# A convolution and a gated two-layer product on one core: the second product in 26 block products in place of 20, with some block sums on GpSimd

## The chip, the core and the metric

The kernel runs on one core of a Trainium2 chip. The core has TensorE (PE, matrix products into PSUM), VectorE (DVE), ScalarE (ACT), GpSimd (POOL) and SyncE (SP, which issues DMAs). The metric is device time in microseconds (us) of one execution, as the median of the runs. The kernel before takes 2314.07 us (three runs, 2314.03 to 2314.65).

## The reference

```python
# x: 8 x 4096 x 192, weight: 8 heads x 7 taps, w_in: 192 x 2048, w_out: 2048 x 192
w = softmax(weight, axis=-1)                   # per head
conv[b, s, c] = sum_k w[head(c), k] * x_pad[b, s + k, c]     # causal, 7 taps
h = conv.reshape(32768, 192) @ w_in
g = h * (1.0 / (1.0 + np.exp(-1.702 * h)))
out = g @ w_out                                # 32768 x 192, float32
```

A depthwise causal convolution of 7 taps, a product up to 2048 features, the quick gelu g = h·sigmoid(1.702h), and a product back to 192. All is float32.

## The kernel before

The tokens are worked off in 32 chunks ("big" in the code, `N_BIG`), each of 1024 tokens: 512 (`TOK`) from one half of the batch and 512 from the other. The first chunk is computed plainly, mixed with the preparation of the weights (`first_step`, `second_first`). Each of the other 31 passes through these stages:

1. **Convolution of the next chunks.** `transpose_x` turns the input with VectorE. The channels come in three blocks c = 0, 1, 2 of 64. Block 0 is done by ScalarE (`tap_times`: seven scaled copies) and GpSimd (`add_tap`: six adds of 128x512); blocks 2 and 1 are done by VectorE (`conv`, seven operations each). Then GpSimd forms eight sums of 128x256 (`sums_c`), and DMAs copy each half of the partitions to the other half (`cross`).
2. **Two hidden stages**, `hidden` with v = 0 and 1: h = conv · w_in by a fast scheme with 21 products (`TERMS`), each of four TensorE instructions in the trace. ScalarE copies PSUM banks into `room` (`copy2`), VectorE combines them (`sum2`), and ScalarE writes the gelu into `g` (`gelu`).
3. **The second product**, `second`: `w_out` and `g` are cut into blocks and multiplied by a scheme with 20 block products, each over five rows of 128 features; the sixteenth row is multiplied plainly. TensorE works in rounds: three matmuls with 32 columns of weights each make a step of the main product, and a fourth, beside them in the last 32 columns, a step of one of the side products (`side_product`, `go`). A round is 256 tokens wide, and there are 81 per chunk. VectorE forms sums of blocks of g (128x1280) ahead of the rounds that read them, and joins the products (96x256) into the four outputs, which it turns (`turn`) into `osbs` for the store.

Each engine works off its own queue in the order in which the program issues it; semaphores tie the queues together. The order within `second` is written out by hand: the sums, `go`, joins and `done` stand in the order of issue. Work that fits between (convolution, transposes) is handed out by `work` with a budget in us, and ScalarE's taps by `next_tap` in the last rounds. All six GpSimd adds of block 0 are issued behind the last of the seven tap copies. `prepare` lists the VectorE and GpSimd work of a chunk, `need` forces what is due. The sums of `w_out` (`w_form`) are made once, at the start, by ScalarE copies (`begin_forms`) and accumulating DMAs that GpSimd issues (`add_forms`).

What the steps of the prediction touch: L494 (VectorE's conv step), L501 (ScalarE's tap), L505 (GpSimd's tap add), L388 and L390 (`add_up`, GpSimd's `sums_c`), L607 (`copy2`), L611 (`sum2`), L598 and L600 (gelu), L867 (every matmul of `second`), L881 (copy of a side product), the sums of g in `hidden` and `second` (L649 to L930), the joins (L908 to L972) and L819 (`turn`).

## Time and profile before

| | |
|---|---|
| median of three runs | 2314.07 us (2314.03 to 2314.65) |
| span of the profiled execution | 2312.2 us, 1.87 below that median; its own time is not listed apart |
| granted TensorE clock | 1.000 |
| TensorE, matmul | 2304.8 us busy |
| VectorE | 2005.1 us busy, 2819 instructions |
| ScalarE | 1376.9 us busy, 2554 instructions |
| GpSimd | 432.4 us busy, 451 instructions |
| matmuls of the hidden stages (L577) | 852.5 us into the slots, 405.4 us into the sums |
| sums of g, 128x1280, VectorE | 16 lines x 31, 1.48 us each |
| conv step, 128x512, VectorE (L494) | x378, 0.803 us in the mean |
| tap copy, 128x512, ScalarE (L501) | x180 into g, 0.719 us |
| tap add, 128x512, GpSimd (L505) | x180, 1.360 us in the mean |
| sum of the convolution, 128x256, GpSimd (L390) | x180, 0.732 us |

The span runs from the first to the last instruction of one execution. An engine's busy time is what its instructions cover; matmuls overlap in the pipeline, so TensorE's says only that it always had work. A line of the timeline gives the start and the duration in us, the engine, the source line, the operation, and the tiles it writes and reads with their shapes; a bracket at its end gives the idle time before it and what ended that. The duration of an instruction runs from where its engine took it up to its end, so a wait for a resource inside the instruction is part of it.

### The profile page before, as it was taken

Reading aid. Unit: us, or ns where it says so; the run is one execution under the profiler, and the core shown is the slowest. Engines: PE = TensorE matmul, PEld = TensorE weight load, DVE = VectorE, ACT = ScalarE, POOL = GpSimd, SP = SyncE. Lnnn points to the kernel's source line nnn. Section 1 sums busy time; section 2 is a strip of 40 time slices with the busy share of each in tenths; the row PEclk is TensorE's granted clock in tenths of the full one; section 3 lists DMA queues with packets and bytes.
Section 4 is the critical chain, followed back from the end, with each engine's and each line's share of the span. In section 5 each row is a group of like instructions: output and inputs, shape, how many; then the busy total and the mean of one; then the engine's idle time right before and its main releaser. Section 6 shows DMA issues by size and latency. Waiting matters only on the chain.

```text
span 2312.2 us, 60320 instructions
## 1 busy us (share of the span) xinstructions
PE 2304.8 (100%) x25982; PEld 1217.8 (53%) x25982; DVE 2005.1 (87%) x2819; ACT 1376.9 (60%) x2554; POOL 432.4 (19%) x451
## 2 busy tenths in 40 slices
PE   9999999999999999999999999999999999999999
PEld 5355555555555555555555555555555555555556
DVE  8898889888898888898888988889888898888877
ACT  7555665566655556555566555665565655556644
POOL 0311222102221022211122211222102221022200
PEclk9999999999999999999999999999999999999999
DMA  8632322223221233112331132321223321231010
GB/s 185 121 67 60 70 52 47 56 57 70 65 48 43 57 70 70 42 43 58 70 70 43 44 69 57 70 53 45 57 57 70 68 45 43 57 70 45 17 43 16
DMA packets 199899, 137.99 MB, mean 60 GB/s; under 512 B 109008, under 2 KB 190544, under 8 KB 195664
## 3 DMA queue, kind: packets, MB, share of 16 engines
q1 hardware_dynamic: 197072, 130.98, 25.7%
q0 software_dynamic: 1728, 2.95, 0.8%
q8 instruction: 204, 3.34, 0.6%
q14 instruction: 63, 0.52, 0.1%
q10 hardware_dynamic: 832, 0.20, 0.0%
HBM read 53.15 MB, written 25.17 MB: 34 GB/s over the span
## 4 chain that ended last, share of the span: by engine, by line
PE 99%; ACT 0%; DVE 0%; DMA 0%; issue 0%; SPq 0%; DVEq 0%; ACTq 0%
PE slot L577 35%; PE slot L867 33%; PE sums L577 16%; PE sums L867 14%; PE slot L746 2%; DMA xin<-in_x_dram 0%; ACT conv_t L1029 0%; DVE xt L471 0%; DVE conv_t L494 0%; SPq L99 0%; ACT conv_t L354 0%; ACT conv_t L353 0%; DVE osbs L819 0%; ACT conv_t L523 0%; ACT conv_t L1025 0%
## 5 line engine op out<-in xcount | busy, mean ns | idle before, releaser
L577 PE MATMUL slot<-conv_t,w_in_s 64*128 64x512 f32 x3740 | 852.5, 590 | 0.3 <-DVE w_in_s L373 0.3
L867 PE MATMUL slot<-g,w_form 128*32 128x256 f32 x6700 | 772.5, 379 | 0.0
L577 PEld LDWEIGHTS slot<-conv_t,w_in_s 64*128 64x128 f32 x3740 | 369.0, 187 | 432.1 <-issue 386.9
L505 POOL TENSOR_TENSOR conv_t<-conv_t,g 128x512 f32<-128x512 f32 x180 | 244.8, 1360 | 1448.6 <-ACT conv_t L501 1436.8
L867 PEld LDWEIGHTS slot<-g,w_form 128*32 128x32 f32 x6700 | 399.6, 110 | 134.9 <-ACT g L598 23.5
L867 PE MATMUL sums<-g,w_form 128*32 128x256 f32 x3530 | 461.8, 379 | 0.0
L867 PE MATMUL slot<-g,w_out_s 128*32 128x256 f32 x4432 | 442.0, 379 | 0.0
L577 PE MATMUL sums<-conv_t,w_in_s 64*128 64x512 f32 x1660 | 405.4, 591 | 0.3 <-DVE w_in_s L373 0.3
L600 ACT ACTIVATE g<-room 128x1024 f32<-128x1024 f32 x310 | 324.5, 1073 | 90.9 <-DVE room L611 90.9
L494 DVE SCALAR_TENSOR_TENSOR conv_t<-xt,cw,conv_t 128x512 f32<-128x512 f32 (+1 forms) x390 | 309.3, 793 | 10.1 <-ACT conv_t L492 3.2
L867 PEld LDWEIGHTS slot<-g,w_out_s 128*32 128x32 f32 x4432 | 226.0, 110 | 97.5
L867 PEld LDWEIGHTS sums<-g,w_form 128*32 128x32 f32 x3530 | 233.3, 110 | 65.6
L607 ACT COPY room<-slot 128x512 f32<-128x512 f32 x434 | 231.5, 602 | 57.3 <-PE slot L577 57.3
L577 PEld LDWEIGHTS sums<-conv_t,w_in_s 64*128 64x128 f32 x1660 | 165.7, 187 | 189.1 <-issue 154.1
L598 ACT ACTIVATE g<-slot 128x512 f32<-128x512 f32 x334 | 179.7, 590 | 88.8 <-PE slot L577 88.8
L881 ACT COPY room<-slot 32x256 f32<-32x256 f32 x245 | 89.8, 367 | 205.8 <-PE slot L867 200.2
L867 PE MATMUL sums<-g,w_out_s 128*32 128x256 f32 x1706 | 205.3, 379 | 0.0
L867 PE MATMUL slot<-room,w_form 128*32 128x256 f32 x2340 | 182.1, 379 | 0.0
L611 DVE TENSOR_TENSOR room<-slot,room 128x512 f32<-128x512 f32 x248 | 156.1, 680 | 20.4 <-ACT room L607 20.4
L611 DVE TENSOR_TENSOR room<-room,sums 128x512 f32<-128x512 f32 x124 | 79.1, 679 | 70.2 <-PE sums L577 70.2
L611 DVE TENSOR_TENSOR room<-room,slot 128x512 f32<-128x512 f32 x124 | 79.1, 678 | 64.5 <-PE slot L577 64.5
L607 ACT COPY room<-sums 128x512 f32<-128x512 f32 x186 | 100.0, 591 | 58.8 <-PE sums L577 58.8
(212 smaller groups left out, 2665.5 us busy)
## 6 DMA issues: line engine op xcount, KB each, us to landing
xin<-in_x_dram SPq DMA_DIRECT2D x240, 180.0 KB, 4.1
conv_t<-conv_t SPq DMA_DIRECT2D x62, 512.0 KB, 6.2
out_dram<-osbs SPq DMA_DIRECT2D x186, 128.0 KB, 2.6
conv_t<-conv_t SPq DMA_DIRECT2D x62, 256.0 KB, 3.1
conv_t<-conv_t SPq DMA_DIRECT2D x62, 64.0 KB, 4.5
xin<-in_x_dram SPq DMA_DIRECT2D x16, 160.0 KB, 3.3
w_form<-w_out_s POOLq DMA_DIRECT2D x7, 240.0 KB, 4.1
osbs<-in_moe_w_out_dram SPq DMA_DIRECT2D x2, 768.0 KB, 8.3
```

Source lines behind the costliest of these rows:

```text
L494: vec.scalar_tensor_tensor(out=dst, in0=src, scalar=tap, in1=dst, op0=ALU.mult, op1=ALU.add)
L505: nc.gpsimd.tensor_add(dst, dst, tap_home(big, k))
L577: nc.tensor.matmul(slot[h], w_in_s[halves[h], a, v * P : (v + 1) * P], src, start=first, stop=True, skip_group_check=True,)
L598: act.activation(g[:, n, i + h, :], src[h], AF.Gelu_apprx_sigmoid)
L600: act.activation(g[:, n, i : i + 2, :], src, AF.Gelu_apprx_sigmoid)
L607: act.copy(bank(dst, h), bank(src, h))
L611: op(*(bank(t, h) for t in (dst, a, b)))
L746: nc.tensor.matmul(chunk(bank, c), w[:, chunk_cols(c)], t, start=first and i == 0, stop=not more and i == len(steps) - 1, skip_group_check ...
L867: nc.tensor.matmul(dst, w, t, start=first, stop=last, skip_group_check=True)
L881: act.copy(to, d)
```

## The change

- **The second product** goes by 26 products of blocks of four rows (16 = 4·4 rows, no row left over), and takes 78 rounds per chunk where it took 81. `g` is laid out anew as blocks of 4 rows by 256 tokens; `gelu` writes it with other strides. 19 of the products are main, 6 side, and one (form 8) is split between the two.
- **The sums of g** are 28 per chunk, of 128x1024 each, in place of 16 of 128x1280. Six of them are in-place adds on GpSimd ("acc" in the lists; the description given with the change speaks of eight): one in the second hidden stage and five inside the second product. The other 22 stay on VectorE: five in the hidden stage (`EARLY_G`), 17 in the second product.
- **The order** within `second` is a list, `PLAN`, that is worked off item by item: "sum" and "join" go to VectorE, "acc" to GpSimd, "seed" is a ScalarE copy of a value into another PSUM place, "go" n issues n rounds of the main product begun by "main", with the side product begun by "side" beside it, "tap" issues one convolution tap, "cross" one piece of the DMA copies.
- **Convolution block 2** moves from VectorE to ScalarE and GpSimd (`prepare_taps`, `tap`): 14 taps and 12 adds per chunk where there were 7 and 6. Each add is issued right behind its copy, into one of four places. Seven taps are issued in the last rounds of the second product, seven in the first hidden stage (`taps_at`). VectorE keeps block 1.
- **The DMA copies** `cross` of a chunk are cut into pieces of three blocks, issued at six places of `PLAN`.
- **The sums of w_out** are 19 GpSimd adds and six ScalarE negations at the start, with no accumulating DMAs.

```diff
-    NS, ND = 3, 5
-    assert len(PAIRS) * 4 == NF == NS * ND + 1
-    g = consts.tile([P, 2, NF, TOK], F32)
-    ROW = {1: 2, 2: 0, 3: 1}
-    COL = {1: (0, 0), 2: (0, 1), 3: (1, 1), 4: (1, 0)}
+    NG = 4
+    assert len(PAIRS) * 4 == NF == NG * NG
+    g = consts.tile([P, NG, 2, 2, NG, T], F32)
     def block(r, j):
-        n, o = COL[j]
-        i = ND * ROW[r]
-        return g[:, n, i : i + ND, o * T : (o + 1) * T]
-    def rest(j):
-        n, o = COL[j]
-        return g[:, n, NF - 1 :, o * T : (o + 1) * T]
+        return g[:, r, j // 2, j % 2, :, :]
+    def row(n, i):
+        return g[:, i // NG, n, :, i % NG, :]
...
+    ROOMS = (1, 2, 3)
+    SPOTS = 2 + len(ROOMS)
+    KEPT = (4, 0)
+    def spot(i):
+        if i >= SPOTS:
+            return block(*divmod(i - SPOTS, NG))
+        flat = osbs[:, i * BLK : (i + 1) * BLK] if i < 2 else room[:, ROOMS[i - 2], :]
+        return flat.rearrange("p (k t) -> p k t", k=NG)
+    KEPT_LATE, TAP_SPOTS = 3, (16, 15)
...
+    SUMS_O = [
+        (8, 7, "+", 6), (9, 5, "+", 7), (10, 2, "+", 6), (11, 3, "-", 5), (12, 3, "-", 6), (13, 3, "+", 7),
...
-    def begin_forms(items):
-        for dst, src, sign in items:
-            if sign == 1:
-                act.copy(form(dst), of_form(src))
-            else:
-                act.mul(form(dst), of_form(src), -1.0)
     def add_forms(items):
-        for dst, src in items:
-            nc.gpsimd.dma_start(out=form(dst), in_=of_form(src), accum_op=ALU.add)
+        for dst, a, op, b in items:
+            add_up(form, dst, a, op, b, eng=nc.gpsimd)
+    def end_forms():
+        add_forms(SUMS_O_LATE)
+        for i in TURN_O:
+            act.mul(form(i), form(i), -1.0)
...
-    def tap_times(big, k):
-        dst = tap_home(big, k) if k else own(big)[:, 0:2, :]
-        act.mul(dst, conv_src(big, 0, k), cw[:, 0, k : k + 1])
-    def add_tap(big, k):
-        dst = own(big)[:, 0:2, :]
-        nc.gpsimd.tensor_add(dst, dst, tap_home(big, k))
+    def tap(big, c, k):
+        dst = own(big)[:, 2 * c : 2 * c + 2, :]
+        home = tap_home(big, c, k) if k else dst
+        act.mul(home, conv_src(big, c, k), cw[:, c, k : k + 1])
+        if k:
+            nc.gpsimd.tensor_add(dst, dst, home)
...
+    def cross_now(early, big, b0, b1):
+        if early or big == 1:
+            cross(big, b0, b1)
+        else:
+            pieces.extend((big, b, min(b + 3, b1)) for b in range(b0, b1, 3))
+    def cross_piece():
+        if pieces:
+            cross(*pieces.pop(0))
...
-        yield from convs(2, 0) if big == 1 else convs(2, 1)
+        yield from convs(2, 0) if big == 1 else convs(1)
...
-        for k in (*range(1, K), 0):
-            yield "", 1.0, lambda k=k: tap_times(big, k)
-        for k in range(1, K):
-            yield "", 0.0, lambda k=k: add_tap(big, k)
+        for c in (0, 2):
+            for k in range(K):
+                yield "", 1.0, lambda c=c, k=k: tap(big, c, k)
...
+        dst = g[:, i // NG, n, :, i % NG : i % NG + 2, :]
...
+        def taps_at(n):
+            for _ in range(0 if v else n):
+                next_tap()
+        def early(i):
+            for item in EARLY_G[i] if v else ():
+                sum_g(*item)
         if v:
             pe(z, 7, first=True)
             give(True, big)
-        pe(sums, 12)
-        copy2(k15, sums)
-        pe(x, 5, 17)
+        if v:
+            pe(sums, 12)
+            copy2(k15, sums)
+            pe(x, 5, 17)
+        else:
+            pe(x, 5)
+            pe(sums, 12)
+            copy2(k15, sums)
+            pe(x, 17)
+            taps_at(1)
...
-            vec.tensor_add(t_s, block(2, 1), block(2, 4))
-            vec.tensor_sub(block(2, 1), block(2, 1), block(3, 1))
-        work(2.6 if v else 1.2)
+        early(1)
+        if not v or big == 1:
+            work(1.2)
         pe(sums, 13)
...
+        early(2)
...
-        if v:
-            vec.tensor_sub(t_a, block(2, 3), block(3, 3))
+        early(3)
...
-        if v:
-            vec.tensor_add(block(2, 3), block(2, 2), block(2, 3))
-            vec.tensor_sub(t_8, t_s, block(3, 1))
...
+    EARLY_G = [
+        [(6, 6, "-", 10)], [(1, 7, "-", 6), (1, 1, "-", 11)], [(0, 5, "+", 6), (8, 0, "acc")],
+        [(2, 9, "-", 0)],
+    ]
+    PLAN = [
+        ("side", 13, 16, "k0"), ("main", 1, 5, "p2", 1), ("go", 4), ("sum", 14, 14, "-", 18),
+        ("main", 16, 10, "p3", 0), ("go", 2), ("sum", 7, 8, "-", 7), ("go", 1), ("cross",), ("go", 1),
+        ("main", 0, 14, "p0", 1), ("go", 1), ("sum", 5, 11, "-", 19), ("go", 1), ("seed", "p4", "p2", 1),
+        ("go", 1), ("seed", "k1", "p3", 1), ("go", 1), ("sum", 8, 8, "-", 16), ("seed", "p5", "k1", 1),
+        ("side", 19, 1, "k1"), ("acc", 14, 13), ("main", 18, 0, "p2", 0), ("go", 3), ("sum", 6, 8, "-", 6),
+        ("go", 1), ("main", 5, 8, "p1", 0), ("go", 1), ("sum", 4, 5, "-", 10), ("go", 1), ("cross",),
+        ("seed", "k2", "p2", 1), ("go", 2), ("sum", 0, 0, "+", 5), ("main", 14, 2, "p2", 0), ("go", 2),
+        ("acc", 15, 4), ("go", 1), ("join", "k3", "p1", "+", "k0"), ("go", 1), ("sum", 11, 7, "+", 11),
+        ("side", 11, 17, "k0"), ("main", 23, 4, "p5", 0), ("go", 3), ("sum", 8, 6, "-", 13),
+        ("seed", "k4", "p2", 1), ("go", 1), ("cross",), ("seed", "p2", "k3", 1), ("main", 17, 6, "p1", 0),
+        ("go", 1), ("sum", 5, 20, "-", 12), ("go", 1), ("seed", "k5", "p5", 1), ("go", 1), ("acc", 7, 10),
+        ("go", 1), ("sum", 20, 20, "-", 11), ("main", 22, 11, "p2", 0), ("go", 2), ("seed", "k6", "p1", 1),
+        ("go", 1), ("seed", "p1", "k2", 1), ("go", 1), ("join", "k7", "k1", "+", "k6"),
+        ("side", 8, 8, "k1", 2, 4), ("main", 2, 5, "p4", 0), ("go", 1), ("sum", 13, 18, "+", 4), ("go", 2),
+        ("cross",), ("sum", 6, 9, "-", 5), ("go", 1), ("acc", 12, 9), ("main", 20, 0, "p1", 0), ("go", 2),
+        ("join", "k2", "k7", "-", "p4"), ("side", 6, 13, "k8"), ("go", 1), ("join", "k2", "k2", "-", "p2"),
+        ("go", 1), ("sum", 15, 15, "-", 16), ("main", 9, 6, "p4", 0), ("go", 3),
+        ("join", "k9", "p1", "+", "k5"), ("go", 1), ("join", "k10", "p0", "-", "k9"), ("main", 3, 15, "p2", 0),
+        ("go", 1), ("cross",), ("acc", 18, 14), ("go", 1), ("seed", "p1", "k1", 1), ("sum", 5, 7, "+", 15),
+        ("tap",), ("go", 2), ("main", 21, 7, "p2", 0), ("go", 1), ("sum", 6, 14, "+", 6), ("go", 1), ("tap",),
+        ("side", 7, 20, "k1"), ("go", 2), ("sum", 6, 6, "-", 17), ("main", 10, 14, "p0", 0), ("go", 2),
+        ("tap",), ("seed", "k5", "p2", 1), ("cross",), ("join", "k10", "k10", "+", "k8"), ("go", 2),
+        ("join", "p2", "p4", "+", "k3"), ("main", 8, 8, "p1", 0, 0, 2), ("go", 1),
+        ("join", "k8", "k9", "+", "k5"), ("tap",), ("go", 1), ("join", "k8", "k7", "-", "k8"),
+        ("main", 4, 6, "p4", 0), ("go", 1), ("turn", 1, 0, 1, "k10"), ("go", 1),
+        ("join", "k3", "p1", "+", "k6"), ("go", 1), ("tap",), ("join", "k3", "p0", "-", "k3"), ("go", 1),
+        ("join", "k6", "k0", "-", "p0"), ("side", 8, 5, "k0"), ("main", 15, 12, "p2", 0), ("go", 2),
+        ("join", "k7", "k4", "-", "p4"), ("go", 1), ("tap",), ("join", "k7", "k7", "+", "k3"), ("go", 1),
+        ("join", "k2", "k2", "-", "k1"), ("main", 12, 18, "p3", 0), ("go", 1), ("turn", 0, 0, 0, "k7"),
+        ("go", 1), ("join", "k6", "k6", "+", "p4"), ("tap",), ("go", 1), ("turn", 1, 1, 1, "k2"), ("go", 1),
+        ("turn", 1, 0, 0, "k6"), ("store", 0, 0), ("main", 24, 19, "p5", 0), ("go", 2), ("final",),
+        ("join", "k1", "p3", "-", "k3"), ("go", 1), ("turn", 0, 0, 1, "k1"), ("store", 0, 1), ("go", 1),
+        ("join", "k2", "p2", "-", "k4"), ("turn", 0, 1, 1, "k2"), ("store", 1, 1),
+        ("join", "k1", "p5", "+", "k5"), ("turn", 0, 1, 0, "k1"), ("join", "k8", "k8", "+", "k0"),
+        ("turn", 1, 1, 0, "k8"), ("store", 1, 0),
+    ]
+    def sum_g(dst, a, op, b=None):
+        if op == "acc":
+            nc.gpsimd.tensor_add(spot(dst), spot(dst), spot(a))
+        else:
+            add_up(spot, dst, a, op, b)
+    SIDE_HALF = (0, 0, 1, 0, 1, 0, 1)
...
+        mains, sides = (bs[0], bx[0], by[0]), (bx[1], bs[1], by[1])
+        side, count = [], [0]
...
+        def begin_side(f, s, to, *ks):
+            steps = product(f, s, *ks)
+            for c in range(NC):
+                turns, i = divmod(count[0], NC)
+                h = SIDE_HALF[turns]
+                count[0] += 1
+                dst = sides[i][n3:, h * T : (h + 1) * T]
+                for k, (w, t) in enumerate(steps):
+                    end = k == len(steps) - 1
+                    side.append((dst, w[:, chunk_cols(c)], t, k == 0 and h == 0, end and chunk(value(to), c)))
+        def begin_main(f, s, to, first, *ks):
+            now.update(steps=product(f, s, *ks), to=value(to), first=bool(first))
+        def go(n):
+            for _ in range(n):
+                w, t = now["steps"].pop(0)
                 for c in range(NC):
+                    one_matmul(chunk(now["to"], c), w[:, chunk_cols(c)], t, now["first"], not now["steps"])
+                now["first"] = False
                 d, ws, ts, st, to = side.pop(0)
                 one_matmul(d, ws, ts, st, to is not False)
                 if to is not False:
                     act.copy(to, d)
+        def seed(dst, src, sign):
+            if sign == 1:
+                act.copy(value(dst), value(src))
+            else:
+                act.mul(value(dst), value(src), -1.0)
+        def out_turn(m, n, o, src):
+            turn(m, n, blocks(value(src)), slice(o * T // Q, (o + 1) * T // Q))
+        def out_store(n, o):
+            if last:
+                queues = (nc.sync, nc.scalar) if o else (nc.scalar, nc.sync)
+                store(big, n, o, queues + queues[0:1])
+                return
+            stored[n] += 1
+            if stored[n] == 2:
+                store(big, n)
+        ops = dict(
+            sum=sum_g, acc=lambda d, a: sum_g(d, a, "acc"), main=begin_main, side=begin_side, go=go, seed=seed,
+            join=lambda d, a, op, b: add_up(value, d, a, op, b), turn=out_turn, store=out_store,
+            tap=next_tap, cross=cross_piece, final=final,
+        )
+        for item in PLAN:
+            ops[item[0]](*item[1:])
+        assert not side and not now["steps"] and count[0] == NC * len(SIDE_HALF)
+        while pieces:
+            cross_piece()
```

## The prediction

> **What bounds the kernel now.** I read the page's busy shares, the chain that ended last, stretches of one chunk, and then single instructions where GpSimd meets VectorE.
>
> The page, parts 1 and 4:
>
> ```profile
> PE 2304.8 (100%) x25982; PEld 1217.8 (53%) x25982; DVE 2005.1 (87%) x2819; ACT 1376.9 (60%) x2554; POOL 432.4 (19%) x451
> ...
> PE 99%; ACT 0%; DVE 0%; DMA 0%; issue 0%; SPq 0%; DVEq 0%; ACTq 0%
> ```
>
> TensorE is never idle and is the whole chain, so a TensorE round taken away is time saved, as long as the operands still arrive. Whether they do is read from the second-product stage (988.2 to 1023.2 us is one). Busy time by engine in two stretches, the stage and the change to the next chunk:
>
> ```profile
> 988.00:1022.00 34.00, 34.00 (x630) 20.46 (x632) 32.59 (x45) 16.04 (x36) 0.00 (x0) 1.00 0.17 41
> 1022.00:1033.00 11.00, 11.00 (x71) 5.12 (x64) 9.59 (x15) 5.97 (x12) 9.97 (x9) 1.00 0.35 74
> ```
>
> In the stage VectorE (third engine column) is busy 32.59 of 34.00 us and GpSimd (the fifth) not at all. So TensorE is the bound there with VectorE 4% behind it. GpSimd works only in the second stretch. The chunk's start shows what the two do to each other (timeline: start, us, engine):
>
> ```profile
> 98.11 0.77 DVE L494 SCALAR_TENSOR_TENSOR conv_t<-xt,cw,conv_t 128x512 f32<-128x512 f32 x1
> 98.41 1.60 POOL L505 TENSOR_TENSOR conv_t<-conv_t,g 128x512 f32<-128x512 f32 x1
> 98.92 1.64 DVE L494 SCALAR_TENSOR_TENSOR conv_t<-xt,cw,conv_t 128x512 f32<-128x512 f32 x1
> 100.09 1.60 POOL L505 TENSOR_TENSOR conv_t<-conv_t,g 128x512 f32<-128x512 f32 x1
> ...
> 1022.40 1.28 POOL L505 TENSOR_TENSOR conv_t<-conv_t,g 128x512 f32<-128x512 f32 x1 [49.19 <-ACT conv_t L501]
> 1022.63 1.34 DVE L959 TENSOR_TENSOR room<-room 96x256 f32<-96x256 f32 x1
> 1023.89 0.41 DVE L964 TENSOR_TENSOR spare<-spare,slot 96x256 f32<-96x256 f32 x1
> ```
>
> The reader should see three things. A VectorE operation with two SBUF inputs waits for a running GpSimd add: L959, of a shape that takes 0.415 us elsewhere (L949), takes 1.34 and ends at 1023.97, 0.29 after the add's end (1022.40+1.28). One with a PSUM input does not (L964, 0.41 us, during the next add). And they take turns: the add at 98.41 is 1.60 long, not 1.28; it ends at 100.01 and the conv behind it at 100.56. The next add ends at 101.69, so one such pair, each of 512 elements, takes 1.68 us.
>
> **The change, part by part.** Durations are from this execution, span 2312.2 us; the median run is 1.87 us above it, which I leave as it is. One chunk of before: two successive chunks on the chain are 142.71 us apart (690.76 to 833.47), so 71.36. There are 31.
>
> *Rounds.* 81 rounds take 988.2 to 1023.2, 35.0 us: 0.432 each. Three fewer: −1.30 us a chunk, −40.2 in all.
>
> *VectorE's list.* Sixteen sums of 1280 elements (1.48 us each; 1.40 from start to start in a row, L896 to L897) become 22 of 1024. The 2048-element sums (L762, 2.28) and 1280 give 1.05 ns an element, so 1.22 alone and 1.135 in a row. 16×1.40=22.4 becomes 22×1.135=25.0: +2.6. Seven convs leave, 0.48+6×0.75: −5.0. Joins stay 21, turns 8. Taken alone VectorE gains 2.4 us.
>
> *GpSimd's list.* The lists hold six block adds of 1024 (the description speaks of eight): one in the hidden stage, five inside the second product. GpSimd rows of 256 (0.73) and 512 (1.28) give 2.1 ns an element, so 2.35 us. Tap adds go from 6 to 12 (1.28 each). In sum 14 us becomes 6×2.35+12×1.28+8×0.73=35.3 of about 70: room enough by itself.
>
> *The turn-taking.* This is what decides. Of the 1.68 us of a pair, a conv alone is 0.76 (L494 in a row), so an add of 512 costs VectorE 0.92; an add of 1024 carries 512×2.1 ns=1.08 more: 2.0. From below the unscaled 0.92 bounds it, from above the whole add with its gap, 2.43. I take 2.0, the measured turn with the measured slope.
>
> Now count VectorE's list in order against the rounds that wait for it. It opens with the last k18 pair (1.2). The five adds become ready while VectorE has sums queued.
> - Round 32 (form 22, spot 11) needs sum 11=7+11: 1.2 + 8 sums (9.1) + join k3 (0.4) + two adds (4.0), less 0.4 since the join reads PSUM and runs beside an add: 14.3 us. The round is due at 13.8.
> - Round 36 needs 5=20−12: two more sums and the third add, 18.6 against 15.6.
> - Round 42, the side product of spot 13: sums 20 and 13, join k7, the fourth add: 23.3 against 18.1.
> - Round 48 needs 15=15−16. In all 1.2 + 14×1.135 + 4 joins (1.6) = 18.7, and 5×2.0 less 1.1 beside three PSUM joins = 8.9: 27.6 against 20.7, **6.9 us late**.
>
> TensorE is in order, so this is a stall of 6.9 us in every chunk. Without the adds VectorE would be 2.0 us ahead at the same place. With 0.92 an add the lateness is 1.5; with 2.43 and nothing beside, 10.2. After round 48 the joins before round 62 (main of spot 6 into p4) wait behind tap adds: 0.5 us. Later sums have rounds to spare.
>
> [...]
>
> *Hidden stages.* VectorE's tail of joins and turns ran 4 us into the next stage before (last turn at 1026.82, stage at 1023.2). Now the late joins meet tap adds, so it runs 4 to 5 us over; the copy into k15 waits for the join that reads k5 in the same room. Seven taps (0.72 each, L501) go into ScalarE's queue in the first hidden stage, ahead of copies that free PSUM; ScalarE was busy 11.95 of 18.00 us there, 5.0 more fit. Waiting behind a tap are copies of 1.07 us, of which TensorE takes notice only when a bank is reused. I take 0.6 us a chunk, with 0 (all covered by the 6 us idle on ScalarE) and 2.5 (the tail and two tap waits bare) as ends. The conv of block 1 meets six tap adds (0.92 each), covered by the waits VectorE had in that stage (1.20+0.82+1.84).
>
> *At no cost.* Copies of values: 11 seeds for 5, +6×0.37=2.2 us on ScalarE, busy 16.04 of 34. The cross copies become 12 DMAs from 6, spread over the stage; SP issues one in 0.52 us, the last lies some 28 rounds (12 us) before use and landing takes 6.2 at most. If late, the first terms of the next chunk would wait. The gelu's new strides move as many elements as before.
>
> *Start.* 12 accumulating DMAs and 13 ScalarE copies become 19 GpSimd adds of 384 elements, about 1.0 us each, beside VectorE's convs. TensorE had no idle there (10.00 of 10.00 in each stretch after 20 us), so no gain; I take +3, ends 0 and +10.
>
> Sum: −1.30+6.9+0.5+0.6=+6.7 a chunk, ×31=+208, +3: 2314+211=**2525 us**.
>
> **The rivals.**
> - *The adds hide.* If GpSimd's adds don't hold up VectorE's sums, the stage has no stall but the 0.5: 2314−40+16+3 = 2293, or 2277 without these; say 2285. For it: GpSimd idle, VectorE ahead by 2.0. Against it: every pair seen. It decides if an add costs VectorE under 0.8 us (18.7+5×0.8−1.1 is 0.9 past round 48, and with the 0.5 that makes up the 1.3 saved); half-size adds cost 0.92.
> - *VectorE first.* If a full VectorE queue keeps its turn and the adds slip in only at PSUM joins, sums come in time but 15+=4 waits until about 21, and round 48 is 3.5 late: 31×(3.5+0.5+0.6−1.3)=+102, 2419. Against it: at 98.41 the waiting add came ahead of a conv issued directly behind another.
> - *ScalarE behind GpSimd.* The hidden stages' 2.5 in full: +59, 2585.
> - *The clock.* The single waits come to 2.5 us (rounds 32 to 36). The granted clock is 1.00 throughout, and no TensorE idle above 1.44 is in the trace. If a wait halved the clock for as long again as it lasted, the two longest (2.5 and 2.1) would lose half of that each, 2.3 a chunk: +71, 2596, and about 2640 should the waits be half as long again. [...]
>
> **How the numbers follow.** Forecast 0.64, ScalarE 0.12, clock 0.05, VectorE first 0.10, adds hide 0.09. The likeliest's own range, from the price of an add between 1.6 and 2.4, is 2460 to 2610. The range 2400 to 2640 takes in VectorE first and both worse cases, and leaves out the faster case and the 0.92 end. 0.2% (4.6 us) is about what three runs can tell: faster 0.09, same 0.01, slower 0.90.
>
> **What would show it.** TensorE waits in the stage of about 7 us a chunk, put down to VectorE's sums at rounds 32 to 48; 1024-element VectorE sums at 1.2 us alone and near 3.3 behind an add; adds of 2.35, longer where they wait. Wrong if those sums stay at 1.2 us while an add runs, or if TensorE stays above 99% busy.

## The result and the profile after

The changed kernel takes **2628.15 us** (median of four runs, 2626.98 to 2628.88), the kernel before 2314.10 beside it: a ratio of **1.136 with an interval of 1.134 to 1.137**. The forecast was slower, 2525 us with a range of 2400 to 2640; the direction and the mechanism hold, and 103 us are missing. The measured time lies above the 2460 to 2610 that the forecast gave for its likeliest case. The profiled execution took 2627.74 us, its span 2625.8.

The page of the changed kernel, parts 1 and 4, to be set against the two lines of before:

```profile
PE 2376.8 (91%) x25238; PEld 1358.0 (52%) x25238; DVE 2395.1 (91%) x2794; ACT 1545.0 (59%) x2942; POOL 1301.0 (50%) x824
...
PE 51%; DVE 38%; issue 4%; ACT 2%; ACTq 0%; DVEq 0%
```

TensorE has work for 91% of the span and not for all of it, and the chain that ended last now lies on VectorE for 38%. The same two stretches of one chunk as before, the second product and the change to the next chunk (the columns are TensorE, its weight loads, VectorE, ScalarE, GpSimd, clock, DMA):

```profile
1044.87:1078.87 34.00, 27.79 (x492) 16.17 (x495) 33.83 (x26) 12.35 (x30) 18.01 (x6) 1.00 0.15 38
1078.87:1088.70 9.83, 7.78 (x140) 4.07 (x132) 9.27 (x19) 5.58 (x11) 6.52 (x5) 1.00 0.01 3
```

VectorE is busy 33.83 of 34.00 us there, with fewer instructions than before (26 for 45): part of the "busy" time is waiting inside an instruction. GpSimd is busy 18.01 us where it did nothing. What TensorE waits for, summed over the execution (line waited at, engine and tile waited for: us, times, longest):

```profile
PE slot L928 <- DVE g L389: 67.9, 44, 2.5
PE sums L928 <- DVE g L389: 40.0, 16, 2.5
PE sums L928 <- DVE room L387: 26.3, 15, 1.8
PE slot L928 <- DVE room L387: 24.5, 14, 1.8
PE slot L928 <- ACT room L953: 24.1, 17, 1.7
```

"g" are the block sums, "room" the joins. One stage on TensorE's timeline, only the lines with a wait (start, us, and in the bracket the idle time and what ended it); the stage begins at 1044.87:

```profile
1059.51 1.93 PE L928 MATMUL slot<-g,w_form 128*32 128x256 f32 x32 [0.62 <-DVE g L387]
1063.95 0.42 PE L928 MATMUL slot<-g,w_out_s 128*32 128x256 f32 x3 [2.50 <-DVE g L389]
1068.86 0.38 PE L928 MATMUL slot<-g,w_form 128*32 128x256 f32 x1 [1.69 <-ACT room L953]
1070.23 1.28 PE L928 MATMUL slot<-g,w_form 128*32 128x256 f32 x19 [0.35 <-DVE room L389]
1073.21 0.42 PE L928 MATMUL slot<-g,w_out_s 128*32 128x256 f32 x3 [1.05 <-DVE g L389]
1079.76 0.42 PE L928 MATMUL slot<-g,w_out_s 128*32 128x256 f32 x3 [0.30 <-DVE slot L387]
1086.90 0.42 PE L928 MATMUL slot<-g,w_out_s 128*32 128x256 f32 x3 [1.76 <-DVE room L387]
```

In order these are rounds 32, 36, 42, 44, 48, 62 and 74. Round 48 starts 28.34 us into the stage; 48 rounds of 0.432 are 20.74. So it is 7.6 us late, of which the brackets name 6.21: each stop costs some 0.25 us more than its bracket says, because idle time is counted from the modelled end of the last matmul (0.38 us long), while in a running stream the next four matmuls start 0.22 us after the four before them (1045.33 and 1045.55).

What VectorE and GpSimd do to each other (timeline, us):

```profile
1050.36 3.47 POOL L904 TENSOR_TENSOR g<-g 128x1024 f32<-128x1024 f32 x1 [9.39 <-DVE g L389]
1051.50 3.40 DVE L389 TENSOR_TENSOR room<-g 128x1024 f32<-128x1024 f32 x1
1054.83 1.21 DVE L387 TENSOR_TENSOR osbs<-osbs,g 128x1024 f32<-128x1024 f32 x1
1054.98 3.29 POOL L904 TENSOR_TENSOR g<-g,room 128x1024 f32<-128x1024 f32 x1 [1.16 <-DVE room L389]
1056.30 3.07 DVE L387 TENSOR_TENSOR g<-g 128x1024 f32<-128x1024 f32 x1
...
1064.98 2.60 DVE L387 TENSOR_TENSOR room<-room 96x256 f32<-96x256 f32 x1
...
1067.67 0.37 ACT L953 COPY room<-slot 32x256 f32<-32x256 f32 x1 [5.80 <-DVE room L387]
```

A sum that takes 1.21 us with no add running takes 3.40 and 3.07 behind one. An add takes 3.29 and 3.47 here (3.22 to 3.47 for the five of this stage), and 2.37 in the row of those that met nothing (form g<-g,osbs, 31 of them). The join at 1064.98, 0.41 us by itself, waits for the fourth add and ends at 1067.58; the ScalarE copy of a side product into the place that this join reads waited 5.80 us for it, and TensorE, whose next side product needs the PSUM place, stopped 1.69 us at round 42.

### The profile page after: what moved, and what is told of

It is laid out like the page before. It is cut to its first block, busy times and chain, and to the rows that moved or that the text cites. A ratio compares the mean times of both kernels' runs of the same rounds, so it can differ in the third digit from the quotient of the medians.

```text
span 2625.8 us, 60414 instructions
## 1 busy us (share of the span) xinstructions
PE 2376.8 (91%) x25238; PEld 1358.0 (52%) x25238; DVE 2395.1 (91%) x2794; ACT 1545.0 (59%) x2942; POOL 1301.0 (50%) x824
## 4 chain that ended last, share of the span: by engine, by line
PE 51%; DVE 38%; issue 4%; ACT 2%; ACTq 0%; DVEq 0%
PE slot L578 29%; DVE g L389 18%; PE sums L578 13%; PE slot L928 6%; DVE room L387 6%; DVE room L389 6%; DVE g L387 4%; PE sums L928 2%; DVE room L619 1%; DVE osbs L387 1%; DVE osbs L846 1%; ACT g L494 1%; DVE slot L387 0%; ACT room L957 0%; ACT room L953 0%
## 5 line engine op out<-in xcount | busy, mean ns | idle before, releaser
L578 PE MATMUL slot<-conv_t,w_in_s 64*128 64x512 f32 x3740 | 956.3, 595 | 16.6 <-issue 8.8
L496 POOL TENSOR_TENSOR conv_t<-conv_t,g 128x512 f32<-128x512 f32 x360 | 491.4, 1365 | 515.3 <-ACT g L494 500.6
L578 PEld LDWEIGHTS slot<-conv_t,w_in_s 64*128 64x128 f32 x3740 | 497.2, 187 | 353.4 <-issue 233.9
L389 DVE TENSOR_TENSOR g<-g 128x1024 f32<-128x1024 f32 x372 | 606.9, 1659 | 3.8 <-ACT g L604 0.7
L904 POOL TENSOR_TENSOR g<-g 128x1024 f32<-128x1024 f32 x124 | 390.6, 3150 | 411.9 <-DVE g L389 308.8
L578 PE MATMUL sums<-conv_t,w_in_s 64*128 64x512 f32 x1660 | 495.7, 594 | 0.3 <-DVE w_in_s L372 0.3
L928 PE MATMUL slot<-g,w_out_s 128*32 128x256 f32 x4080 | 330.5, 389 | 96.6 <-DVE g L389 67.9
L494 ACT ACTIVATE g<-xt,cw 128x512 f32<-128x512 f32 x360 | 258.0, 743 | 2.2
L486 DVE SCALAR_TENSOR_TENSOR conv_t<-xt,cw,conv_t 128x512 f32<-128x512 f32 (+1 forms) x210 | 224.0, 1067 | 7.7 <-ACT conv_t L484 3.0
L953 ACT COPY room<-sums 32x256 f32<-32x256 f32 x217 | 79.3, 365 | 205.2 <-PE sums L928 202.5
```

The source lines that it names most:

```text
L389: eng.tensor_sub(v(dst), v(a), v(b))
L486: vec.scalar_tensor_tensor(out=dst, in0=src, scalar=tap, in1=dst, op0=ALU.mult, op1=ALU.add)
L494: act.mul(home, conv_src(big, c, k), cw[:, c, k : k + 1])
L496: nc.gpsimd.tensor_add(dst, dst, home)
L578: nc.tensor.matmul(slot[h], w_in_s[halves[h], a, v * P : (v + 1) * P], src, start=first, stop=True, skip_group_check=True,)
L904: nc.gpsimd.tensor_add(spot(dst), spot(dst), spot(a))
```

## The experiments

"After" is the changed kernel with 2628.15 us; each edit is one to it. Beside them the kernel before took 2314.3 to 2314.4. All but the last two were run once; the four runs of after lie 1.9 us apart, and the smallest difference read below is 7 us. The first four separate the adds from the tap additions.

**The five adds left out.** The one in the hidden stage stays.

```diff
-            sum=sum_g, acc=lambda d, a: sum_g(d, a, "acc"), main=begin_main, side=begin_side, go=go, seed=seed,
+            sum=sum_g, acc=lambda d, a: None, main=begin_main, side=begin_side, go=go, seed=seed,
```

> Leaves out the five GpSimd block adds inside the second product (the output is not the reference's); the sixth, in the hidden stage, and all else stay. Theory (each add holds VectorE's next sum with two SBUF inputs for about 2.3 us, and the sums then reach rounds 32 to 48 too late): TensorE's waits at those rounds go, and the wait for a join in the last rounds (1.75 us) goes too, since VectorE is then early. 7.6 + 1.9 us a chunk less, about 2335 us (2320 to 2355). Rival (VectorE's list of 22 sums is too long by itself, adds or not): the waits stay, over 2560. Rival (the tap adds of convolution block 2 do it): little changes, over 2560.

Measured: 2390.7 us, −237. A chunk is 73.28 us (996.10 to 1069.38) and not 80.9: 7.6 us less, as expected for this part. The waits of rounds 32 to 48 are all gone. The miss is what stayed, the wait of round 74, here in full:

```profile
PE sums L928 <- DVE room L387: 26.4, 15, 1.8
PE slot L928 <- DVE room L387: 24.6, 14, 1.8
```

So it isn't a rest of the lateness of round 48: it has a cause of its own. Between this run and after, VectorE's rows of block sums and joins differ by 331.6 us (L389 g<-g 606.9 for 448.5, L387 room<-room 191.3 for 95.1, L387 g<-g 167.8 for 110.3, L389 room<-g 57.3 for 37.8): 10.7 us a chunk. Not all of it is the adds. Set against each other operation by operation (VectorE's order is the same in both), 9.8 us a chunk lie in the sums and the join that meet an add: 2.16 to 2.21 for three of the adds, 1.86 and 1.40 for the two beside which one and two joins from PSUM ran. The other 0.97 is a join that, being late, now meets the first tap addition (1.51 us at 1077.39; 0.42 in this run). So an add costs VectorE **2.18 us where no join from PSUM runs beside it, and 1.96 in the mean of the five**.

**The five adds on VectorE**, nothing left out:

```diff
-            ... acc=lambda d, a: sum_g(d, a, "acc"), ...
+            ... acc=lambda d, a: add_up(spot, d, d, "+", a), ...
```

> The same five adds, put on VectorE in the same place of its list: the whole computation, with 5 x 1.135 = 5.7 us more VectorE work a chunk and 11.8 us less on GpSimd. Theory: an add then costs VectorE 1.14 us and not the 2.0 measured in the mean (10.1 us in five); the sum of round 48 ends about 23.9 us into the stage and not 28.3, 3.2 us late and not 7.6; the wait in the last rounds stays. About 2495 us (2470 to 2530). Rival (the length of VectorE's list decides): 5.7 us a chunk more, about 2800.

Measured: 2520.3 us. A chunk is 78.0 us, or 76.4 in every third or fourth (77.4 in the mean). Moving the five adds to the idle engine cost 108 us over doing them on the engine that was the limit: VectorE paid 1.96 us in the mean for an add that it does itself in 1.135.

**The tap additions left out** (all twelve of a chunk):

```diff
 if k:
-    nc.gpsimd.tensor_add(dst, dst, home)
+    pass
```

> Leaves out the twelve GpSimd tap adds of every chunk (convolution blocks 0 and 2 are wrong); ScalarE's tap copies, the block adds and all else stay. Theory: the waits at rounds 32 to 48 lie before the first tap add and stay (7.6 us a chunk); the wait in the last rounds (1.9) and the 0.8 us in the hidden stages go, and at the start about 9 us, where the sums of w_in took turns with tap adds. About 2535 us (2515 to 2570). Rival (the tap adds are what holds VectorE up): below 2400.

Measured: 2550.7 us, −77. The waits of rounds 32 to 48 are as they were (0.67, 2.50, 1.69, 0.35, 1.05), and the wait of round 74 is gone. A chunk is 2.4 us shorter, and the first second product begins 7.8 us earlier.

**Adds of half the elements:**

```diff
+            ... acc=lambda d, a: nc.gpsimd.tensor_add(spot(d)[:, 0:2, :], spot(d)[:, 0:2, :], spot(a)[:, 0:2, :]), ...
```

> Each of the five adds covers only half of its block, 512 elements and not 1024 (the output is wrong). Theory (VectorE is held for as long as the add reads): 2.1 ns x 512 = 1.08 us less for each, 5.4 us a chunk, about 2460 us (2440 to 2500). Rival (a fixed price for each handover): no change, 2600 to 2630. Rival (VectorE's list): no change.

Measured: 2453.8 us. Half the adds' length takes away 174 of the 237 us. The half adds cost VectorE 4.2 us a chunk by the same count, and the chunk is 2.0 longer than without adds (75.3 for 73.3): the rest is covered by what VectorE has in hand, some 2.1 us (the forecast put that at 2.0 before round 48). The other halves cost 5.6 more, and the chunk is 5.6 longer: all of it is lateness.

The next four ask how the price comes about and what else is in it.

**The adds as accumulating DMAs**, nothing left out:

```diff
+            ... acc=lambda d, a: nc.gpsimd.dma_start(out=spot(d), in_=spot(a), accum_op=ALU.add), ...
```

> The computation is whole. The five adds become accumulating DMAs of 512 KB that GpSimd issues, so that neither VectorE nor GpSimd touches the elements. If the adds' price is the time in which VectorE and GpSimd take turns, all of it goes and the time is that of the run without the adds, 2391 us (2375 to 2415), with the waits of rounds 32 to 48 gone and the 1.76 us wait of round 74 still there. The rounds allow a landing of about 7 us between an add and what reads it; the 240 KB accumulations at the start of the kernel before landed in 4.1 to 5.3 us, so 512 KB may take 6 to 9. Rival: a landing or the issuing itself is too slow; then TensorE waits for a sum behind a DMA and the time stays above 2430.

Measured: 2389.0 us, the time of the run without the adds. The same sums are made, by DMAs and not by adds on GpSimd, and the price is gone. The DMA view of this run (KB each, median us from issue to landing):

```profile
g<-g POOLq DMA_DIRECT2D x124, 512.0 KB, 5.7
```

**Each add in two halves**, nothing left out:

```diff
+            ... acc=lambda d, a: [nc.gpsimd.tensor_add(spot(d)[:, i : i + 2, :], spot(d)[:, i : i + 2, :], spot(a)[:, i : i + 2, :]) for i in (0, 2)], ...
```

> The computation is whole. Each of the five adds is made as two of 512 elements, one behind the other. If VectorE pays the length of GpSimd's add whatever its pieces are (turns whole instruction by whole instruction), the five cost VectorE about 10 us a chunk again, only spread over two sums each: 2615 us (2590 to 2635). Rival: each handover has a price of its own, about 0.5 us: five more of them make 2.5 us a chunk and 2690. Second rival: VectorE gets its sum in between and only half an add stands in front of it: as with adds of half the size, 2454.

Measured: 2575.6 us, below the lowest value of either full-price theory and far above the third. Its timeline:

```profile
1039.30 2.26 POOL L974 TENSOR_TENSOR g<-g,room 128x512 f32<-128x512 f32 x1
1040.35 2.30 DVE L389 TENSOR_TENSOR g<-g 128x1024 f32<-128x1024 f32 x1
1041.53 2.24 POOL L974 TENSOR_TENSOR g<-g 128x512 f32<-128x512 f32 x1
...
1046.99 1.48 DVE L387 TENSOR_TENSOR room<-room 96x256 f32<-96x256 f32 x1
1048.15 3.72 POOL L974 TENSOR_TENSOR g<-g 128x512 f32<-128x512 f32 x1
1048.40 1.21 DVE L387 TENSOR_TENSOR g<-g,room 128x1024 f32<-128x1024 f32 x1
1049.53 1.21 DVE L389 TENSOR_TENSOR g<-g 128x1024 f32<-128x1024 f32 x1
```

The turns are of whole instructions: half an add, a sum, half an add, a sum (the first three rows end at 1041.56, 1042.65 and 1043.77). Most sums that meet one pay about 1.1 us now (2.30 for 1.21), about twice as often. Operation by operation the ten halves cost VectorE 9.6 us a chunk where the five whole adds cost 9.8, so a handover has no large price of its own. That a chunk is 1.7 us shorter all the same goes with what meets what: the joins pay no more to the tap additions than without any adds (0.97 us a chunk more in after), and the waits fall elsewhere, 0.51 us at round 74 and 2.17 at round 62. How much each of these is worth was not tried. The price of 2.18 for a whole add of 2.37 us agrees with such turns. Who goes first is another question: the last section has a place where the turns are not one and one.

**Convolution block 2 back on VectorE**, nothing left out:

```diff
-        yield from convs(2, 0) if big == 1 else convs(1)
+        yield from convs(2, 0) if big == 1 else convs(2, 1)
...
-        for c in (0, 2):
+        for c in (0,):
```

> The computation is whole. The convolution of block 2 goes back to VectorE (four taps in the hidden stage of every chunk, 2.76 us by their rows), and the six tap additions a chunk that GpSimd made for it go; the second product stays as changed. If the convolution's move costs through GpSimd's additions beside VectorE's joins, the time falls to that of the run without any tap additions, 2551 us (2540 to 2580): the wait of round 74 goes, and VectorE has 3.0 us idle in the first hidden stage besides what the tap additions took from it. Rival: VectorE was too full for the convolution, and TensorE now waits in the hidden stage: 2.8 us a chunk more than without the additions, about 2635, and so the move was worth making.

Measured: 2788.4 us, 160 more than after. That expectation had counted four taps; a block has seven, 5.04 us a chunk (0.48 and six of 0.76), and the two hidden stages take 42.0 us for 37.0. VectorE had no room for them: besides all the old waits, TensorE now stops in the first hidden stage, 28 times for up to 3.9 us, for VectorE's L619 (`sum2`):

```profile
PE slot L578 <- DVE room L619: 50.5, 14, 3.9
PE sums L578 <- DVE room L619: 47.0, 14, 3.6
```

The wait of round 74 is unchanged, since the six tap additions that run beside the last joins are those of block 0. So, given this second product, the move of block 2 was a gain; the rival's sign was right and its size too small.

**One join earlier.** p5, which round 74 writes, is the other half of the PSUM bank of p4, and the last reader of p4 was `k6 = k6 + p4`:

```diff
-        ("join", "k7", "k4", "-", "p4"), ("go", 1), ("tap",), ("join", "k7", "k7", "+", "k3"), ("go", 1),
+        ("join", "k7", "k4", "-", "p4"), ("join", "k6", "k6", "+", "p4"), ("go", 1), ("tap",), ("join", "k7", "k7", "+", "k3"), ("go", 1),
...
-        ("go", 1), ("join", "k6", "k6", "+", "p4"), ("tap",), ("go", 1), ("turn", 1, 1, 1, "k2"), ("go", 1),
+        ("go", 1), ("tap",), ("go", 1), ("turn", 1, 1, 1, "k2"), ("go", 1),
```

> The computation is whole. In the plan of the second product one join, k6 = k6 + p4, is issued three VectorE operations earlier, right behind the other join that reads p4; it needs nothing newer than that one. If round 74 waits because p5 shares its PSUM bank with p4 and the last reader of p4 stands behind joins that take turns with GpSimd's tap additions, the 1.76 us wait goes with the 0.2 us that each stop costs besides: about 1.9 us in 31 chunks, 2569 us (2562 to 2590). Rival: round 74 waits for VectorE as a whole, and the order of the joins is nothing to it: 2628 within 5 us.

Measured: 2582.6 us, −45.5 or 1.47 a chunk, and this wait is no longer in the list (after: 26.3 + 24.5 us, 1.75 in each of 29 chunks). The second product is 2.0 us shorter (41.9 for 43.9), the wait and its stop, but the hidden stages behind it take 0.4 us more (37.36 for 36.99). So the wait was for one reader of a bank, delayed by joins that took turns with the tap additions (0.97 and 1.50 us at 1083.79 and 1084.69, where a join alone is 0.41). p4 and p5 are the two halves of one PSUM tile of 128x512 (`value`), and in after the first matmul that writes the one starts at 1086.90, 0.06 us after the last join that reads the other has ended.

**The start.** Two runs, each with one part. In the first the `next_tap` of `second_first`, which issue seven taps, are taken out, so that all taps of chunk 2 come in the next hidden stage (and use the places of the later chunks), and `end_forms` keeps the negations alone, which `need("forms")` issues right before the second product:

```diff
-        next_tap()
-        next_tap()
         for i in range(0, len(rows22), 2):
...
-            todo.append(("forms", 0.0, end_forms))
+            todo.append(("late sums", 0.0, lambda: add_forms(SUMS_O_LATE)))
+            todo.append(("forms", 9.0, end_forms))
```

> The computation is whole. At the start alone: the tap additions of chunk 2 are not made beside VectorE's sums of w_in but in the next chunk's first hidden stage, and the six negations of w_out's sums stand on ScalarE's queue right before the second product of chunk 1 and not in its hidden stage, while the late sums are issued as before. If these two set the 8.79 and 7.57 us waits and the halved clock behind them, the first second product begins some 15 to 20 us earlier, at 135 to 140 us of the span instead of 154.9, and the time is 2609 us (2606 to 2615). Rival: the sums of w_out on GpSimd are too late in any place; then the wait moves to the first second product and the time is within 6 us of 2628.

In the second the sums of w_out are copies and accumulating DMAs:

```diff
-            add_up(form, dst, a, op, b, eng=nc.gpsimd)
+            if op == "+":
+                act.copy(form(dst), form(a))
+                a = b
+            else:
+                act.mul(form(dst), form(b), -1.0)
+            nc.gpsimd.dma_start(out=form(dst), in_=form(a), accum_op=ALU.add)
```

> The computation is whole. Only the once-made sums of w_out are changed: each is a ScalarE copy and an accumulating DMA, and GpSimd adds nothing there. If the start's second wait (7.57 us) comes from GpSimd being late with these sums, it goes with the halved clock behind it, while the first one (8.79 us, VectorE's sums of w_in beside the tap additions) stays: 2617 us (2612 to 2622). Rival: GpSimd's sums delay VectorE from 60 to 80 us of the span, where VectorE gets through 14 operations and not 24, and the first wait is owed to that too: then most of the 23 us goes, 2608. Second rival: the copies and the landings are as late, 2628 within 5 us.

Measured: 2618.1 us with the first edit, 9 more than expected, and 2621.1 with the second, in the expected range but not for the expected reason. In after the two waits are these (timeline of TensorE and ScalarE):

```profile
106.79 1.31 PE L578 MATMUL slot<-conv_t,w_in_s 64*128 64x512 f32 x2 [8.79 <-issue]
138.15 2.56 PE L578 MATMUL slot<-conv_t,w_in_s 64*128 64x512 f32 x4 [7.57 <-ACT room L615]
...
136.69 0.52 ACT L433 ACTIVATE w_out_s<-w_out_s 128x384 f32<-128x384 f32 x1 [6.85 <-POOL w_out_s L389]
```

The first edit shortens them to 2.58 and 2.28 us; the first second product begins at 143.4 us (after: 154.9, before: 131.9). The second edit shortens the first wait to 2.87 and lengthens the other to 9.60, because ScalarE's negation now waits 7.62 us for a landing DMA instead of GpSimd. So my reading of the second edit was the wrong way round: it was the first wait that shrank. With the first edit the first chunk afterwards is 2.4 us longer (83.36 for 81.00), which takes part of the gain back. The 8.79 us have two sources, GpSimd's w_out sums beside VectorE from 60 to 80 us and its tap additions beside VectorE's w_in sums near 100 (either alone leaves 2.6 to 2.9); the 7.57 us come from a ScalarE negation that stands in the queue ahead of a copy which frees a PSUM bank, whoever makes the sums.

**All the mends together**, nothing left out: adds as DMAs, the join earlier, both edits of the start, and `p2 = p4 + k3` ahead of `k10 = k10 + k8` against the wait of round 62.

> The computation is whole. All the mends together: the five adds as accumulating DMAs, k6 = k6 + p4 three operations earlier, p2 = p4 + k3 ahead of k10 = k10 + k8 (the 0.30 us wait of round 62), the sums of w_out by copies and DMAs, their negations right before the second product, chunk 2's tap additions out of the stretch of the w_in sums. From 2389 us with the adds as DMAs: less 31 times 1.9 (59), less 31 times 0.5 (15), less 15 to 23 at the start: 2296 us (2285 to 2320), so just below the 2314 of before. Rival: with TensorE no longer stopped VectorE is the limit of the chunk and a new wait stands in a later round: 2330 to 2380, and the kernel before stays ahead.

Measured: 2337.6 us (four runs, 2337.3 to 2337.7), ratio to before 1.010 (1.008 to 1.012). The expectation was 42 us too low. The time lies where the rival had it, but no new wait stood in a later round: a chunk is 71.93 us (1103.20 to 1175.13), the wait of round 62 is still 0.29, that of round 74 is 0.42, and the start still costs 7.9 us (139.75 for 131.89). The swap at round 62 did nothing because `p2 = p4 + k3` had been idle 2.88 us behind a ScalarE copy that stood behind tap multiplications. The last run moves that copy ahead of the tap, puts three taps between the rounds behind round 48, and takes out the last three of the list:

```diff
-        ("tap",), ("seed", "k5", "p2", 1), ("cross",), ("join", "p2", "p4", "+", "k3"), ("go", 2),
+        ("seed", "k5", "p2", 1), ("cross",), ("join", "p2", "p4", "+", "k3"), ("tap",), ("go", 2),
...
-        ("go", 1), ("sum", 15, 15, "-", 16), ("main", 9, 6, "p4", 0), ("go", 3),
+        ("go", 1), ("sum", 15, 15, "-", 16), ("main", 9, 6, "p4", 0), ("go", 1), ("tap",), ("go", 2),
...
-        ("join", "k3", "p1", "+", "k6"), ("go", 1), ("tap",), ("join", "k3", "p0", "-", "k3"), ("go", 1),
+        ("join", "k3", "p1", "+", "k6"), ("go", 1), ("join", "k3", "p0", "-", "k3"), ("go", 1),
...
```

> The computation is whole. As the run with all the mends together (2337.6 us, a chunk of 71.9 us), and two more moves in the plan: ScalarE's copy of p2 to k5 is issued ahead of a tap multiplication, because p2 = p4 + k3 sat 2.88 us behind that copy while ScalarE multiplied a tap (the 0.29 us wait of round 62), and the seven taps of the second product are issued some eight rounds earlier, where VectorE has those 2.88 us and 0.86 us idle, so that GpSimd's additions no longer stand beside the last joins (which take 0.9 to 1.4 us there and not 0.4; the 0.42 us wait of round 74). If both waits go, each with the 0.2 us that a stop costs besides, a chunk is 1.1 us shorter: 2303 us (2298 to 2316), 0.3 to 0.7% below the kernel before. Rival: VectorE's 1024-element sums, now beside the tap additions, come late for the products of rounds 54 to 66, and the time is above 2340.

Measured: 2325.7 us (five runs, 2325.6 to 2325.8), ratio 1.0048 (1.0035 to 1.0062): short of the expectation, and still 0.5% slower than the kernel before. No version here beats it. Its page, and from its timeline the wait that is left:

```profile
PE 2296.1 (99%) x25238; PEld 1344.1 (58%) x25238; DVE 2071.4 (89%) x2794; ACT 1551.6 (67%) x2961; POOL 972.1 (42%) x824
```

```profile
1031.96 0.41 DVE L387 TENSOR_TENSOR room<-room,sums 96x256 f32<-96x256 f32 x1
...
1032.43 0.42 PE L927 MATMUL sums<-g,w_out_s 128*32 128x256 f32 x3 [0.52 <-DVE room L387]
```

Round 62 has no wait any more. Round 74 starts 0.06 us after the join that reads the bank's other half, here "sums", has ended (1032.37). A chunk is 71.54 us: 71.36 less 1.30 for three rounds, plus 0.7 in the hidden stages, plus 0.52 and 0.25 for this stop, is 71.53. By this sum the rounds were worth what they were forecast to be, and the rest eats them. Of the 11 us that this version is behind, some 7 lie in the start (first second product at 139.25 for 131.89).

## Why the prediction was right, and where it was too low

The forecast's terms, per chunk, against what they measured:

| term | forecast | measured | from |
|---|---|---|---|
| three rounds fewer | −1.30 | −1.30 | the sum of the last run's chunk closes with it |
| lateness at round 48 | +6.9 | +7.6 | start of the round, 28.34 for 20.74 |
| round 62 | +0.5 | +0.55 | 0.30 and a stop's 0.25 |
| round 74 | 0 | +2.0 | 1.76 and a stop's 0.25 |
| hidden stages | +0.6 | +0.7 | 1007.87 to 1044.87, 37.0 for 36.3 |
| sum | +6.7 | +9.55 | 852.33 to 1014.15 is two chunks of 80.91; before 71.36 |
| start, once | +3 | +23 | first second product at 154.87 for 131.89 |

The missing 103 us are 31 times 2.85, or 88, and 20 at the start, less 5 for the last two chunks, in which round 74 does not wait (it waits 1.75 us in the other 29).

- **The mechanism** is shown: sums of 1.2 us alone and 3.07 to 3.40 behind an add, adds of 2.37 alone, TensorE waits at rounds 32, 36, 42 and 48 as listed, gone without the adds and gone when a DMA makes them.
- **The price of an add** was mis-sized a little: "I take 2.0, the measured turn with the measured slope". It is 2.18 where no join from PSUM runs beside the add. What the step takes off for such joins, 1.1 in all, is what the rows show (0.32 and 0.78), so the five adds cost 9.8 where 8.9 was forecast. The late rounds came as listed and each somewhat later: rounds 32, 36 and 48 by 0.8, 3.5 and 7.6 us where 0.5, 3.0 and 6.9 were forecast. The measured 2.18 and 7.6 lie between the forecast's 2.0 and 6.9 and its upper bounds of 2.43 and 10.2.
- **Round 42** stopped as due, but by another way than through the sum of spot 13: ScalarE's copy of a side product waited for the join k7 behind the fourth add. The step had the join in its count and not the copy behind it.
- **"Later sums have rounds to spare" failed.** It looked at sums only. Round 74 waits for a join, not a sum: the reader of the other half of a PSUM bank, with GpSimd's tap additions beside it. The forecast priced the tap additions for the joins before round 62 and stopped there.
- **The start lies outside its own ends: "I take +3, ends 0 and +10"**, and it is +23. The step priced GpSimd's w_out sums beside VectorE's convs. It left out that VectorE, delayed there, comes to the w_in sums 9.7 us later (95.10 for 85.37), where it now meets the tap additions of block 0, each issued right behind its copy (the sums take 1.37 to 1.5 us each and not 0.42), and it left out the queue: a negation on ScalarE waiting 6.85 us for GpSimd, in front of a copy for which TensorE waits.
- **Hidden stages** came out as taken. Without the tap additions the two take 36.55 us, so 0.44 of the 0.7 go with these; the other 0.3 stay open. The 2.5 us end and with it the rival "ScalarE behind GpSimd" did not occur there. Its mechanism did, once, at the start.
- **"The adds hide"** fell by the rows of sums. **"VectorE first"** fell as well: the sum at 1051.50 waited for the add that had been taken up 1.14 us earlier. One place in the stage with halved adds shows the other order (last section).
- **The landings of `cross`**, put at 6.2 us at most, take 6.2 in the median of the largest of before (512 KB) and up to 7.7 in its steady chunks; in after no wait of TensorE is put down to one.
- **"The clock"** has its mechanism and not its price. The last section has the numbers.
- **The range** held partly by luck. The likeliest case was to lie between 2460 and 2610, and its upper end is not what the sum gives for an add at 2.4 (2.0 us a chunk more, or 2587). The measured 2628 is inside 2400 to 2640 only because that took in the two worse cases, ScalarE behind GpSimd in the hidden stages and the slow clock, and neither came at its price; round 74 and the start, which filled the space, were not among them.

## What to carry to other kernels

When work goes to an idle engine, price it on the engine that it holds up as well: here the five adds cost VectorE 1.96 us each on GpSimd, 1.135 on VectorE itself, and nothing as accumulating DMAs that land in 5.7 us. Follow a delay past the operation that it hits first, to the joins that free a PSUM bank's other half (1.76 us a chunk here) and to the copies queued behind a waiting instruction (6.85 us at the start), and do it for the start as well as for the steady chunk. A saving of 1.7% in rounds, with the engine behind it only 4% short of being the bound, is eaten here by one stop of half a microsecond a chunk, 0.7 us in the hidden stages and a slower start.

## What the runs showed that had not been expected

The granted clock halves behind 17 of the 31 waits of round 36, each of them 2.50 us long, and costs nothing in the chunk there. In after, in the first of two successive chunks round 36 waits 2.50 us and the clock stays at 1.00; in the next, around the same round (columns as above, the clock is the third from the end):

```profile
1143.00:1145.00 2.00, 0.12 (x4) 0.15 (x8) 1.97 (x2) 0.00 (x0) 0.83 (x2) 1.00 0.00 0
1145.00:1147.00 2.00, 2.00 (x24) 1.31 (x25) 2.00 (x2) 0.00 (x0) 2.00 (x1) 0.53 0.05 8
1147.00:1149.00 2.00, 2.00 (x31) 1.25 (x26) 2.00 (x2) 0.39 (x2) 1.21 (x1) 0.62 0.00 0
```

Round 32 comes 80.93 us after that of the chunk before, and 80.92 before that of the chunk behind: the slow rounds only use up the following wait, and the 1.69 us of round 42 are missing in that chunk.

What decides is where the wait lies. In this trace the granted clock changes only at times that are whole multiples of 3.41 us apart, and it is halved for one such step when TensorE was idle for about 2 us of the step before. The 0.53 and 0.62 above are one half-rate step, from 1145.11 to 1148.52. The wait that ends at 1144.88 lies whole in the step from 1141.70 to 1145.11; that of the chunk before, from 1061.45 to 1063.95, is cut into 1.74 and 0.76 us by the border at 1063.19. Over the 31 second products the wait of round 36 halves the clock 17 times, each time with 2.10 us or more of it in one step, and 14 times it doesn't, with 2.05 or less. Two more dips follow rounds 42 and 44 (1.68 and 0.35 us idle), and those two chunks are 81.4 and 81.2 us long and not 80.9. The run without tap additions has the same 2.50 us waits, but a chunk of 78.53 us is 23 such steps, so the border cuts the wait at nearly the same place in every chunk: no wait of round 36 halves the clock there, and its mean is 0.997 for 0.984.

At the start no wait stands behind that could take it up: the clock is 0.50 for 4.1 us after the wait that ends at 106.79 and for 3.4 us after the one that ends at 138.15, so some 3.7 of the 23 us are the clock's, and 16.4 the two waits themselves.

The turns are not strictly one and one. The half add at 1048.15 above took 3.72 us: it was taken up while a join ran, and two sums (1.21 us each) went before it. That place shows it in each of the 31 chunks (3.72 to 3.73 us). Why VectorE keeps its turn there, and not elsewhere, was not tried.
